# Block-sparse attention and SwiGLU feed-forward on one core: one fixed-order pipeline of key-tile steps in place of head-by-head attention

## The chip, the cores and the metric

The kernel runs on one core of one Trainium2 chip. The metric is the device time in microseconds (us) of one execution. TensorE is the matmul engine (PE in the profile, its weight loads PEld), VectorE is DVE, ScalarE is ACT, GpSimd is POOL. A "step" below is one key tile of 128 keys for one pair of heads and one half (384) of a batch's queries; there are 192 of them. A unit is the 24 steps of one such half batch; there are eight, and the feed-forward of a unit runs during the next one. A bank is a slice of PSUM, the memory that matmuls write to; each product below is written to one bank. A column tile is 32 or 64 of the array's 128 columns, used as a small array with weights of its own. A one-hot matmul has weights that are 1 in one column and 0 elsewhere, so that it sums its moving side into one chosen row. "Half rate" means matmuls at twice their later spacing.

In the feed-forward, gp and vp are the gate and the value product of one of 12 blocks f of d_ff; th is tanh of gp, u or uu is th and gp combined, hp is uu times vp, yp is the output projection and yo its copy. In the changed kernel o_ is the output product of a pair, zw the tile of sums, and norm_a to norm_d are the parts of the normalisation; FHL holds its factors.

## The reference

Attention with a block mask, then RMS norm and a SwiGLU feed-forward over the heads' joined output. Cut to what matters:

```python
B, H, S, D = 4, 8, 768, 64            # fp32 inputs; mask in 32x32 blocks
mask = |blk_i - blk_j| <= 1 | first/last block row or column | 3 sampled blocks per block row
attn = softmax(where(mask, q @ k.T / 8, -1e9));  x = (attn @ v) as [3072, 512]
xn  = x / sqrt(mean(x*x, -1) + 1e-6) * rms_g
out = (silu(xn @ w_gate) * (xn @ w_val)) @ w_out    # d_ff = 1536
```

## The kernel before

Per head, the scores come transposed (keys on partitions), the mask rides along as 24 more rows of K and Q, exp goes to SBUF, and the output product has the exp tile as weights and V with a column of ones as the moving side: 65 columns, of which the last is the softmax sum. The feed-forward (FFN) of batch b-1 is emitted between the heads of batch b. The framework's scheduler decides each engine's order.

```python
# pst (scores): 2 banks; pt: 2; po: 1; pff: gp, vp, yp one bank each
def attn_pair_load(b, hp):
    ...                                       # q, k: fp32 DMA in rows of 256 bytes, cast on VectorE
    for e, (raw_, bf) in enumerate(((qraw, qbf), (kraw, kbf))):
        ...
        for c in range(NC):
            nc.tensor.transpose(out=t_[:, c, :], in_=bf[:, c, :], identity=ident)
        nc.vector.tensor_copy(out=dst[0:D, sl0, :], in_=t_[0:D]...)       # both copies on VectorE
        nc.vector.tensor_copy(out=dst[0:D, sl1, :], in_=t_[64:128]...)

def attn_head(b, h, stage, e):
    for jt in range(NC):
        for ic in range(2):
            nc.tensor.matmul(out=stp, lhsT=KTf[0:64 + NB, sl, jt...], rhs=QTf[0:64 + NB, sl, ic...])
            nc.scalar.activation(out=ExpS[...], in_=stp, func=AF.Exp, scale=SCALE)   # 384 columns
    for it in range(NC):
        for jt in range(NC):
            nc.tensor.matmul(out=opsum[:, it, 0:65], lhsT=ExpS[... 128 wide], rhs=Vp[:, sl, jt, :], ...)
    ...                                       # 1/z, scaling, sums of squares on VectorE

def ffn_gateval(pool, g, f):                  # one gp bank, one vp bank during attention
    ...  # 4 matmuls to gp, 4 to vp
    nc.scalar.activation(out=th, in_=gp, func=AF.Tanh, scale=0.5)
    nc.vector.scalar_tensor_tensor(out=u, in0=th, scalar=1.0, in1=gp, op0=ALU.add, op1=ALU.mult)
    nc.vector.tensor_tensor(out=hp, in0=u, in1=vp, op=ALU.mult)
```

The softmax here doesn't subtract the row's maximum and nothing guards it: scores larger than these inputs give would overflow.

## Time and profile before

| | before |
|---|---|
| time, median | 436.8 us (436.0 to 437.4, 4 runs) |
| start, to the first score matmul | 54 us |
| batch 0, attention alone | 76 us |
| batches 1 to 3 with FFN | 253 us |
| last FFN, 768 tokens | 53 us |

The stretches view of the kernel before gives, for each stretch, its length, then busy time and instructions of each engine, the recorded TensorE clock, DMA share and GB/s. The clock reads 1.00 also where nothing was recorded, and the record of this trace begins only at 104.6 us, so the spacing of matmuls is the surer reading:

```profile
0.00:54.00 54.00, 5.74 (x42) 4.01 (x43) 14.69 (x43) 6.61 (x2) 6.17 (x19) 1.00 1.07 192
54.00:130.00 76.00, 64.52 (x481) 37.53 (x481) 36.60 (x156) 50.76 (x111) 0.00 (x0) 0.88 0.66 129
130.00:383.00 253.00, 241.25 (x2072) 141.88 (x2094) 168.12 (x574) 167.70 (x374) 0.00 (x0) 1.00 0.12 36
383.00:437.00 54.00, 48.72 (x267) 26.35 (x265) 27.03 (x49) 16.58 (x31) 0.00 (x0) 0.96 0.08 30
```

In the third stretch TensorE is busy 95% of the time: it is the bound there. In the first it does almost nothing. The last row ends 0.8 us after the span of 436.2 us. The timeline shows what the start waits for, and the DMA line of the page shows the small packets:

```profile
26.86 0.56 DVE L207 CAST qbf<-qraw 128x768 bf16<-128x768 f32 x1 [23.53 <-DMA qraw<-in_q_dram]
49.62 5.40 ACTq L127 DMA_DIRECT2D QTf<-Qmask  x6
54.31 0.80 PE L232 MATMUL stp<-QTf,KTf 88*128 88x384 bf16 x2 [3.37 <-DMA QTf<-Qmask]
...
DMA packets 82407, 30.80 MB, mean 71 GB/s; under 512 B 76452, under 2 KB 78276, under 8 KB 82372
```

The chain of waits (start, length, what) shows the same matmuls at two speeds, half rate during nearly all of batch 0 and full rate after it:

```profile
60.91 1.89 PE opsum L246 x31
70.88 0.64 PE stp L232 x2
...
140.44 1.08 PE opsum L246 x31
399.45 0.65 PE vp L157 x4
```

Two score matmuls of 384 columns take 0.64 us in batch 0; four value matmuls of 384 columns take 0.65 us later. The costliest groups of the page (busy us, mean ns of one, then idle time before and who ended it):

```profile
L238 ACT ACTIVATE ExpS<-stp 128x384 bf16<-128x384 f32 x384 | 171.1, 491 | 48.4 <-PE stp L232 33.8
L246 PE MATMUL opsum<-Vp,ExpS 128*128 128x65 bf16 x1152 | 76.8, 209 | 1.4 <-ACT ExpS L238 1.2
```

### The profile page before, as it was taken

The page shows a single profiled execution, that of the slowest core. Times are in us where ns is not written, and L with a number is a line of the kernel's source. Part 1 is how long each engine was busy: PE and PEld are TensorE (multiplying, and loading weights), DVE is VectorE, ACT ScalarE, POOL GpSimd, SP SyncE. Part 2 cuts the span into 40 slices and gives each one's busy share as a digit, 9 for nine tenths or more (in the row PEclk, how much of TensorE's full clock was granted, in tenths as well). Part 3 has the DMA queues.
Part 4 walks back from the last instruction along what each step waited for, and adds up shares of the span by engine and source line. Part 5 has one row for each costly group of instructions (what it writes and reads, how often), then busy time and mean ns, then how long its engine had stood idle before and what let it go on. Part 6 is the DMA issues. An engine that isn't in the chain of part 4 may idle for free.

```text
span 436.2 us, 7564 instructions
## 1 busy us (share of the span) xinstructions
PE 360.2 (83%) x2854; PEld 209.8 (48%) x2880; DVE 246.4 (56%) x821; ACT 241.7 (55%) x518; POOL 6.2 (1%) x19
## 2 busy tenths in 40 slices
PE   0002288898879999999999999989999999789996
PEld 0001134554555654655555555546555555345552
DVE  0016534363476862766887648578665566657380
ACT  0003266667676666676777476767773867333331
POOL 5000000000000000000000000000000000000000
PEclk9999999999659999999999999999999999989999
DMA  7999986557470202211310111010001000100101
GB/s 124 208 203 207 221 165 136 99 107 148 90 146 20 54 23 90 62 29 44 94 30 20 44 53 34 2 50 24 2 2 50 24 2 2 73 2 0 74 0 72
DMA packets 82407, 30.80 MB, mean 71 GB/s; under 512 B 76452, under 2 KB 78276, under 8 KB 82372
## 3 DMA queue, kind: packets, MB, share of 16 engines
q1 hardware_dynamic: 79332, 25.18, 26.1%
q0 software_dynamic: 2608, 4.72, 5.9%
q10 hardware_dynamic: 432, 0.44, 0.4%
q8 instruction: 22, 0.36, 0.4%
q14 instruction: 13, 0.11, 0.1%
HBM read 28.31 MB, written 6.29 MB: 79 GB/s over the span
## 4 chain that ended last, share of the span: by engine, by line
PE 71%; ACT 9%; SPq 8%; DVE 7%; DMA 3%; issue 2%; ACTq 0%; DVEq 0%
PE stp L232 17%; PE gp L151 14%; PE vp L157 13%; PE yp L175 13%; PE opsum L246 11%; ACT ExpS L238 7%; SPq L220 3%; SPq L202 3%; PE tqk L213 2%; PE to L280 2%; SPq L199 1%; DVE junk L259 1%; DMA vraw<-in_v_dram 1%; ACT yo L181 1%; DMA QTf<-Qmask 1%
## 5 line engine op out<-in xcount | busy, mean ns | idle before, releaser
L238 ACT ACTIVATE ExpS<-stp 128x384 bf16<-128x384 f32 x384 | 171.1, 491 | 48.4 <-PE stp L232 33.8
L232 PE MATMUL stp<-QTf,KTf 88*128 88x384 bf16 x384 | 126.5, 365 | 15.4 <-ACT ExpS L238 9.4
L165 DVE SCALAR_TENSOR_TENSOR u<-th,gp 128x384 bf16<-128x384 bf16 x96 | 53.0, 552 | 58.9 <-ACT th L163 56.5
L246 PE MATMUL opsum<-Vp,ExpS 128*128 128x65 bf16 x1152 | 76.8, 209 | 1.4 <-ACT ExpS L238 1.2
L246 PEld LDWEIGHTS <-ExpS 128*128 128x128 bf16 x1152 | 56.5, 107 | 44.3 <-issue 24.6
L163 ACT ACTIVATE th<-gp 128x384 bf16<-128x384 f32 x96 | 47.1, 490 | 54.2 <-PE gp L151 53.9
L175 PE MATMUL yp<-wo,hp 128*128 128x512 bf16 x262 | 65.6, 379 | 3.2 <-ACT yo L181 2.6
L169 DVE TENSOR_TENSOR hp<-u,vp 128x384 bf16<-128x384 bf16 x96 | 52.8, 551 | 19.3 <-PE vp L157 12.8
L232 PEld LDWEIGHTS <-KTf 88*128 88x128 bf16 x384 | 39.0, 107 | 30.5 <-issue 14.5
L151 PEld LDWEIGHTS <-wg 128*128 128x128 bf16 x384 | 35.8, 98 | 29.2 <-issue 7.9
L157 PEld LDWEIGHTS <-wv 128*128 128x128 bf16 x384 | 36.2, 98 | 25.2 <-issue 3.0
L213 PE MATMUL tqk<-ident,qbf 128*128 128x128 bf16 x96 | 13.0, 263 | 37.4 <-DVE qbf L207 37.3
L175 PEld LDWEIGHTS <-hp 128*128 128x128 bf16 x288 | 27.7, 97 | 32.2 <-issue 4.5
L181 ACT COPY yo<-yp 128x512 f32<-128x512 f32 x24 | 14.1, 586 | 42.7 <-PE yp L175 40.7
L259 DVE CUSTOM_DVE_ANT_0 junk<-stage,ssq 128x64 bf16<-128x64 bf16 x168 | 36.6, 277 | 0.3
L151 PE MATMUL gp<-xbr_152,wg 128*128 128x384 bf16 x96 | 31.6, 329 | 2.5 <-DVE u L165 1.7
L157 PE MATMUL vp<-xbr_152,wv 128*128 128x384 bf16 x96 | 31.6, 329 | 0.6 <-DVE hp L169 0.3
L151 PE MATMUL gp<-xbr_155,wg 128*128 128x384 bf16 x96 | 31.5, 329 | 0.1
L157 PE MATMUL vp<-xbr_153,wv 128*128 128x384 bf16 x96 | 31.6, 329 | 0.0
L151 PE MATMUL gp<-xbr_153,wg 128*128 128x384 bf16 x96 | 31.6, 329 | 0.0
L157 PE MATMUL vp<-xbr_154,wv 128*128 128x384 bf16 x96 | 31.4, 328 | 0.0
L157 PE MATMUL vp<-xbr_155,wv 128*128 128x384 bf16 x96 | 31.4, 328 | 0.0
(53 smaller groups left out, 235.0 us busy)
## 6 DMA issues: line engine op xcount, KB each, us to landing
qraw<-in_q_dram SPq DMA_DIRECT2D x32, 192.0 KB, 3.7
kraw<-in_k_dram SPq DMA_DIRECT2D x32, 192.0 KB, 4.0
vraw<-in_v_dram SPq DMA_DIRECT2D x32, 192.0 KB, 3.1
out_dram<-yo SPq DMA_DIRECT2D x24, 256.0 KB, 2.0
wg<-in_moe_w_gate_dram POOLq DMA_DIRECT2D x1, 1536.0 KB, 12.8
wv<-in_moe_w_val_dram POOLq DMA_DIRECT2D x1, 1536.0 KB, 18.8
wo<-in_moe_w_out_dram POOLq DMA_DIRECT2D x1, 1536.0 KB, 27.9
KTf<-Kind ACTq DMA_DIRECT2D x6, 36.0 KB
```

What stands on the lines that cost most here:

```text
L151: nc.tensor.matmul(out=gp, lhsT=wg[:, c, f * P:(f + 1) * P], rhs=xbr[c][:, g * TG:(g + 1) * TG], start=(c == 0), stop=(c == DM // P - 1),)
L157: nc.tensor.matmul(out=vp, lhsT=wv[:, c, f * P:(f + 1) * P], rhs=xbr[c][:, g * TG:(g + 1) * TG], start=(c == 0), stop=(c == DM // P - 1),)
L163: nc.scalar.activation(out=th, in_=gp, func=AF.Tanh, scale=0.5)
L165: nc.vector.scalar_tensor_tensor(out=u, in0=th, scalar=1.0, in1=gp, op0=ALU.add, op1=ALU.mult,)
L169: nc.vector.tensor_tensor(out=hp, in0=u, in1=vp, op=ALU.mult)
L175: nc.tensor.matmul(out=yp, lhsT=hprods[(g, f)][:, tt * P:(tt + 1) * P], rhs=wo[:, f, :], start=(f == 0), stop=(f == NF - 1),)
L181: nc.scalar.copy(out=yo, in_=yp)
L213: nc.tensor.transpose(out=t_[:, c, :], in_=bf[:, c, :], identity=ident)
L232: nc.tensor.matmul(out=stp, lhsT=KTf[0:64 + NB, sl, jt * P:(jt + 1) * P], rhs=QTf[0:64 + NB, sl, ic * 384:(ic + 1) * 384], start=True, sto ...
L238: nc.scalar.activation(out=ExpS[:, sle, jt * 2 + ic, :], in_=stp, func=AF.Exp, scale=SCALE,)
L246: nc.tensor.matmul(out=opsum[:, it, 0:65], lhsT=ExpS[:, sle, jt * 2 + it // 3, (it % 3) * P:(it % 3 + 1) * P], rhs=Vp[:, sl, jt, :], start ...
L259: nc.vector.tensor_tensor_reduce(out=junk, in0=stage[:, it, e, :], in1=stage[:, it, e, :], scale=1.0, scalar=(0.0 if h == 0 else ssq[:, b ...
```

## The change

The intent: load q, k, v in long rows and cast them in the DMA; run one exp over 768 columns (both heads of a pair) per step; make V the weights of the output product, so that 384 columns stream and the two heads of a pair fill two column halves of the array; take the softmax sums and the sums of squares by one-hot matmuls into 32-row column tiles; apply both normalisations in one multiply; put the FFN of the former 384 tokens between the steps, so that only 384 tokens are left at the end. A table of steps fixes the order on every engine. Core of the diff, cuts marked:

```diff
+    ctx.enter_context(tc.manual_schedule())            # every engine in emission order
+    ps_s = ...bufs=2   # two score buffers of two banks, lent to transposes and norms too
+    ps_a = ...bufs=1   # "zw" and "acc": sums; output product AND output projection
+    ps_f = ...bufs=1   # gp, vp
 ...
+    def load_w_chunk(i):                               # at steps 5, 9, 13, 17
+        for w, src, mul in ((wg, wgv, 1.0), (wv, wvv, 0.5)):
+            st = wst.tile([P, DM // P, FCH], FP32, name="wstage", tag="wstage")
 ...                                                    # chunk 0: a one-element memset of st on VectorE
+            nc.sync.dma_start(out=st, in_=src[:, :, f0:f0 + FCH])
+            for c in range(DM // P):
+                nc.vector.tensor_scalar(out=w[:, c, f0:f0 + FCH], in0=st[:, c, :],
+                    scalar1=gcol[:, c:c + 1], scalar2=mul, op0=ALU.mult, op1=ALU.mult)
 ...
+        t_ = ps_s.tile([P, 2, 1024], BF16, name="tqk", tag="s")
+        ...                                            # 24 transposes into two column tiles
+        nc.vector.tensor_copy(out=QTe[0:D, sl, :], in_=t_[0:D, 0, 0:S])
+        nc.scalar.copy(out=KTe[0:D, sl, :], in_=t_[0:D, 1, 0:S])
+        nc.vector.tensor_copy(out=QTo[D:P, sl, :], in_=t_[D:P, 0, 0:S])
+        nc.scalar.copy(out=KTo[D:P, sl, :], in_=t_[D:P, 1, 0:S])
 ...
+    def av(n): ...
+        for jt in range(NC):
+            for e in range(2):
+                nc.tensor.matmul(out=o_[64 * e:64 * e + 64, 0:TG],
+                    lhsT=vb[:, 2 * pr + e, jt * D:(jt + 1) * D], rhs=pt_[:, jt, e, :], ...)
+    def zsum(n): ...                                   # 12 matmuls, 4 column tiles
+                    nc.tensor.matmul(out=zwt[u][32 * c:32 * c + 32, :], lhsT=Ez[:, pr, :], ...)
 ...
+        if u == NU - 1:                                # last unit: gate and value in one tile
+            gv = ps_s.tile([P, 2, 512], FP32, name="gv", tag="s")
+            gp = gv[:, 0, 0:TG]
+        ...                                            # th, uu as before
+        vp = ps_f.tile([P, TG], FP32, name="vp", tag="vp") if gv is None else gv[:, 1, 0:TG]
 ...
+    LAG = 8
+        at(s1 + 1, av, n); at(s1 + 2, zsum, n); at(s1 + 4, wsum, n)
+            at(s1 + 4, norm_a, u); at(s1 + 5, norm_b, u); at(s1 + 6, norm_c, u)
+            at(s1 + 7, norm_d, u, 0); at(s1 + 7, norm_d, u, 1)
 ...
+            credit += RATE                             # FFN items spread over the steps by cost
```

## The prediction

> **What bounds the kernel now.** The stretches view cuts the 436.2 us span into four stages.
> (1) 0 to 54 us: TensorE does almost nothing (PE 8.5 of the first 58 us). The timeline shows why: the first qraw is cast at 26.9 us and the first score matmul starts at 54.3 us, behind loads in 256-byte rows (76,452 of 82,407 packets are under 512 B) and behind the mask rows, which go out by DMA at 49.6 us.
> (2) 54 to 130 us: attention of batch 0 alone. Matmuls run at half rate: two score matmuls in 0.64 us, 31 opsum matmuls in 1.89 us; later these cost 0.162 us each and 1.0 us.
> (3) 130 to 383 us: three batches of attention with FFN, about 84 us each, PE 96 to 98% busy.
> (4) 383 to 436 us: FFN of 768 tokens alone, dense (0.65 us per four 384-column matmuls, 0.216 us per yp matmul).
>
> **What the change does to TensorE work.** At the full rate, before needs FFN 187 us, scores 62, opsum 1152 x 0.032 = 37, transposes 16: about 302 us. After keeps the first two. Each AV matmul now streams 384 columns into 64 output rows (384 matmuls), the softmax sums are 384 one-hot matmuls of 32 rows, plus 32 square sums, more transposes (384 of half width) and normalisation matmuls. My estimate rests on column tiles running side by side; the Trainium skill, "TensorE: Matmul & The Clock Gate", Part 3, gives 2.38x for three column tiles; no run here shows it yet. Then AV is about 34 us, the sums 18 + 5, transposes 14, the rest 9: 329 us in all, 27 us MORE than before. Unpaired, it would be about 400 us.
>
> **What it removes.** The start: loads become 1,536-byte rows and the mask rows are copied on chip; I expect the first exp at 12 us instead of 55 (-42). Batch 0 alone: 32 steps, limited by ScalarE (one exp of 768 columns, about 0.75 us from 0.49 for 384 and 0.586 for 512 columns, plus KT and osb copies) and by VectorE, which scales weights in order behind 1.5 MB chunk loads: I expect about 47 us instead of 76 (-29). The tail is half as long: after the last score step, about 41 us including the rest of the former unit, the last norm chain and 23.4 us of FFN. ssq (junk 40 us, accumulator reads 15 us of DVE), the rstd multiply and Sqrt with its table loads (1.28 us each) go, but these were off the critical path in stage 3.
>
> **What it gives back.** In the mixed stage (160 steps) TensorE needs about 1.6 us per step, against the equivalent of 1.5 before. I add 0.25: drains when tile sizes change (skill, "TensorEngine Tiling (Array Packing)", Key Properties; not seen here), single gp and acc banks in a fixed order (gp, tanh 0.49, u 0.55 make a loop of some 2.2 us per f, wanted every 2.3), and score buffers lent to transposes and norms. 1.83 x 160 = 293 us.
>
> Sum: 12 + 47 + 293 + 41 = 393 us.
>
> **What would show it.** Timeline: first exp near 12 us; first tanh near 60; last exp near 350. AV pairs start within some ns of each other, 12 in about 1.1 us, 12 sum matmuls in about 0.6. ACT exp about 0.75 us x192. Stretches: PE over 90% busy from 70 to 350 us. Small packets nearly gone.
>
> **What would make it wrong.** Column tiles running one after another (+65 us: same or slower). Half rate lasting past step 32. VectorE blocked longer by weight chunks. Stalls in the mixed stage of 0.1 us per step are worth 16 us either way.
>
> Chances: faster 0.90, within 2% 0.06, slower 0.04. Eight in ten: 366 to 422 us.

## The result, and the profile after

The changed kernel is correct and slower: 488.95 us (487.49 to 490.25, 4 runs) against 436.78 us (436.01 to 437.44, 4 runs). The ratio is 1.12 (95% interval 1.117 to 1.123). Ratios here are the mean time of one kernel's fast runs over that of the other's of the same rounds, so they are not quite the ratios of the medians quoted.

The stretches of the changed kernel, cut where the first exp starts, where the first tanh (the first FFN work) starts and where the last exp ends:

```profile
0.00:16.50 16.50, 3.27 (x29) 1.76 (x30) 8.97 (x23) 2.87 (x3) 14.36 (x37) 1.00 0.72 95
16.50:82.90 66.40, 39.78 (x278) 16.23 (x277) 29.10 (x77) 33.36 (x45) 15.12 (x22) 0.77 0.65 149
82.90:425.90 343.00, 302.04 (x2211) 152.21 (x2209) 128.02 (x254) 203.91 (x316) 41.80 (x53) 0.98 0.17 32
425.90:488.00 62.10, 40.75 (x217) 19.54 (x215) 19.46 (x39) 11.24 (x23) 1.68 (x2) 0.97 0.07 26
```

Set against the sum in the prediction (12 + 47 + 293 + 41), every stage is longer: 16.5, 66.4, 343.0 and 61.8 us. The start did get much shorter, and small packets are nearly gone. In the mixed stage TensorE stands at 88% busy, and no engine is full. (The clock record begins at 27.2 us here and at 26.2 us in x_fence below, so the 1.00 of the first row says nothing.)

The arithmetic itself behaves as predicted. In the timeline (start, length, instruction), one pair's 12 output matmuls (o_, L262) start at 206.57 and the next matmul at 207.66, 1.09 us later; the 12 sum matmuls (zw, L280) take 0.60 us to the next start:

```profile
206.57 1.17 PE L262 MATMUL o__2023<-pt,vb 128*64 128x384 bf16 x12
207.66 0.82 PE L361 MATMUL gp<-xn,wg 128*128 128x384 bf16 x4
209.40 0.67 PE L280 MATMUL zw<-pt,Ez 128*32 128x384 bf16 x12
210.00 0.82 PE L361 MATMUL gp<-xn,wg 128*128 128x384 bf16 x4
...
DMA packets 22786, 24.02 MB, mean 49 GB/s; under 512 B 1764, under 2 KB 19684, under 8 KB 22756
```

One after another, 12 matmuls of 384 columns would take 12 x 0.1625 = 1.95 us. So the column tiles do run side by side.

What fills the rest of the time is waiting. The waits view (who for whom: total us, times, longest):

```profile
DVE uu L367 <- ACT th L365: 114.8, 96, 6.8
ACT KTe L231 <- DVE QTe L230: 36.2, 16, 11.6
PE gp L361 <- DVE uu L367: 18.9, 35, 2.0
PE gv L375 <- DVE uu L367: 14.0, 12, 1.2
PE s__421 L245 <- ACT KTo L233: 12.4, 1, 12.4
```

Here are three places in the timeline. First, batch 0. VectorE works in order; at 30.74 its one-element memset lets the next chunk's DMA go (issued at 30.83), and then it stands for 6.15 us until that chunk lands. The mask rows and the QTe copy, which the next scores need, sit behind it, and TensorE stands for 12.38 us:

```profile
30.74 0.06 DVE L210 MEMSET wstage<- 1x1 f32 x1
36.95 1.41 DVE L213 TENSOR_SCALAR wv<-wstage,gcol 128x384 bf16<-128x384 f32 x4 [6.15 <-DMA wstage<-in_moe_w_val_dram]
38.39 0.35 DVE L157 COPY KTe<-Kind 32x768 bf16<-32x768 bf16 x1
...
40.30 0.55 DVE L230 COPY QTe<-tqk 64x768 bf16<-64x768 bf16 x1
42.30 0.79 ACT L233 COPY KTo<-tqk 64x768 bf16<-64x768 bf16 x1 [0.63 <-DVE QTo L232]
43.15 0.48 PE L245 MATMUL s__421<-QTe,KTe 88*128 88x384 bf16 x1 [12.38 <-ACT KTo L233]
```

Second, the mixed stage. A pair's four copies run strictly one after another, hopping between two engines. ScalarE is in order too, so from 212.57 to 214.78 it serves only the two KT copies and the hops; a gate product that had started at 212.54 gets its tanh at 214.81, and the scores of 213.35 get their exp at 215.19:

```profile
211.99 0.55 DVE L230 COPY QTe<-tqk 64x768 bf16<-64x768 bf16 x1
212.57 0.79 ACT L231 COPY KTe<-tqk 64x768 bf16<-64x768 bf16 x1 [0.52 <-DVE QTe L230]
213.40 0.56 DVE L232 COPY QTo<-tqk 64x768 bf16<-64x768 bf16 x1 [0.86 <-ACT KTe L231]
213.99 0.79 ACT L233 COPY KTo<-tqk 64x768 bf16<-64x768 bf16 x1 [0.63 <-DVE QTo L232]
214.81 0.49 ACT L365 ACTIVATE th<-gp 128x384 bf16<-128x384 f32 x1
215.19 0.81 ACT L249 ACTIVATE pt<-s__2127 128x768 bf16<-128x768 f32 x1
```

Third, the tail. The value matmuls of the last unit wait for uu, though uu reads only the gate half of the tile and they write the other half. A block f of the FFN takes 2.63 us (447.74 to 450.37), where before took 1.3 us:

```profile
447.74 0.49 ACT L365 ACTIVATE th<-gv 128x384 bf16<-128x384 f32 x1 [2.14 <-PE gv L361]
448.26 0.56 DVE L367 SCALAR_TENSOR_TENSOR uu<-th,gv 128x384 bf16<-128x384 bf16 x1 [0.62 <-ACT th L365]
448.87 0.81 PE L375 MATMUL gv<-xn,wv 128*128 128x384 bf16 x4 [1.17 <-DVE uu L367]
449.52 0.81 PE L361 MATMUL gv<-xn,wg 128*128 128x384 bf16 x4
...
450.37 0.49 ACT L365 ACTIVATE th<-gv 128x384 bf16<-128x384 f32 x1 [2.14 <-PE gv L361]
```

### The profile page after: what moved, and what is told of

It is laid out like the page before. It is cut to its first block, busy times and chain, and to the rows that moved or that the text cites. A ratio compares the mean times of both kernels' runs of the same rounds, so it can differ in the third digit from the quotient of the medians.

```text
span 487.7 us, 6743 instructions
## 1 busy us (share of the span) xinstructions
PE 385.8 (79%) x2730; PEld 189.7 (39%) x2730; DVE 185.6 (38%) x392; ACT 251.4 (52%) x385; POOL 73.0 (15%) x112
## 4 chain that ended last, share of the span: by engine, by line
PE 57%; DVE 15%; ACT 15%; issue 5%; DMA 4%; POOL 2%; POOLq 0%; ACTq 0%; DVEq 0%
PE gp L361 11%; PE yp L389 11%; PE vp L375 7%; DVE uu L367 5%; ACT th L365 5%; PE zw L280 4%; ACT pt L249 3%; ACT KTe L231 3%; DMA wstage<-in_moe_w_val_dram 3%; PE tqk L227 2%; PE gv L375 2%; ACT KTo L233 2%; DVE QTo L232 2%; DVE QTe L230 2%; PE gv L361 2%
## 5 line engine op out<-in xcount | busy, mean ns | idle before, releaser
L367 DVE SCALAR_TENSOR_TENSOR uu<-th,gp 128x384 bf16<-128x384 bf16 x84 | 46.5, 554 | 104.0 <-ACT th L365 104.0
L361 PE MATMUL gp<-xn,wg 128*128 128x384 bf16 x336 | 70.0, 331 | 18.9 <-DVE uu L367 18.9
L375 PE MATMUL vp<-xn,wv 128*128 128x384 bf16 x336 | 69.9, 331 | 1.3 <-DVE hp L378 1.3
L378 DVE TENSOR_TENSOR hp<-uu,vp 128x384 bf16<-128x384 bf16 x84 | 46.6, 554 | 25.5 <-PE vp L375 19.0
L375 PEld LDWEIGHTS <-wv 128*128 128x128 bf16 x384 | 35.6, 98 | 46.9 <-issue 26.5
L245 PEld LDWEIGHTS <-KTo 128*128 128x128 bf16 x192 | 19.4, 101 | 42.8 <-issue 30.8
L231 ACT COPY KTe<-tqk 64x768 bf16<-64x768 bf16 x16 | 12.7, 792 | 36.2 <-DVE QTe L230 36.2
L245 PEld LDWEIGHTS <-KTe 88*128 88x128 bf16 x192 | 19.6, 102 | 26.3 <-issue 10.3
L262 PEld LDWEIGHTS <-vb 128*64 128x64 bf16 x384 | 21.0, 117 | 21.4 <-issue 13.7
L280 PE MATMUL zw<-pt,Ez 128*32 128x384 bf16 x384 | 22.2, 338 | 0.0
L345 DVE TENSOR_TENSOR xn<-osb,fb 128x768 bf16<-128x768 f32 x16 | 14.8, 952 | 16.7 <-PE fb L342 16.6
```

The lines of the kernel that those rows point to most:

```text
L231: nc.scalar.copy(out=KTe[0:D, sl, :], in_=t_[0:D, 1, 0:S])
L245: nc.tensor.matmul(out=s_[:, e, 0:TG], lhsT=KT[0:K, sl, jt * P:(jt + 1) * P], rhs=QT[0:K, sl, ic * TG:(ic + 1) * TG], start=True, stop=True)
L262: nc.tensor.matmul(out=o_[64 * e:64 * e + 64, 0:TG], lhsT=vb[:, 2 * pr + e, jt * D:(jt + 1) * D], rhs=pt_[:, jt, e, :], start=(jt == 0), s ...
L280: nc.tensor.matmul(out=zwt[u][32 * c:32 * c + 32, :], lhsT=Ez[:, pr, :], rhs=pt_[:, 2 * j2 + par, e, :], start=(pr == 0 and j2 == 0), stop ...
L361: nc.tensor.matmul(out=gp, lhsT=wg[:, c, f * P:(f + 1) * P], rhs=xns[u][:, c, :], start=(c == 0), stop=(c == NP - 1))
L367: nc.vector.scalar_tensor_tensor(out=uu, in0=th, scalar=1.0, in1=gp, op0=ALU.add, op1=ALU.mult)
```

## The experiments

Unless it says otherwise, each is one edit to the changed kernel ("after"). All used 3 rounds beside the kernel before on the same chip, and all results are correct except one that is wrong. The stages are read from each trace: first exp; from there to the first tanh; from there to the end of the last exp (mixed); the tail. The last column but one is the trace's span in us; the ratio is to the kernel before, as in the result. A gain in us given below is the difference of two such ratios times 436.7 us, which takes out the small differences between chips. Gains of 3 us are near what these runs can tell: in e4_spread and e10_gpcopy, whose edits act from step 32 on, the exp of step 21 already comes 2.6 and 2.5 us earlier than in the changed kernel.

In e5_norm and the x_ runs the FFN starts two steps later, so some 3 us that the other rows count as mixed stand in their second stage. From the exp of step 32 to the last one, which is the same cut for all, it is 343.8 us in the changed kernel, 324.5 in e5_norm, 324.2 in e9_copies, 308.7 in x_manual, 300.9 in x_hybrid and 301.1 in x_fence.

| kernel | first exp | to first tanh | mixed | tail | span | ratio |
|---|---|---|---|---|---|---|
| predicted | 12 | 47 | 293 | 41 | 393 | |
| after | 16.5 | 66.4 | 343.0 | 61.8 | 487.7 | 1.120 |
| e1_tail | 16.5 | 66.4 | 342.7 | 49.9 | 475.5 | 1.093 |
| e2_auto | 34.6 | 54.8 | 307.4 | 45.2 | 442.0 | 1.017 |
| e3_weights | 16.5 | 50.0 | 345.5 | 61.7 | 473.7 | 1.088 |
| e4_spread | 16.5 | 63.3 | 332.8 | 70.2 | 482.8 | 1.112 |
| e5_norm | 16.5 | 64.6 | 320.5 | 58.7 | 460.3 | 1.061 |
| e7_sums | 16.5 | 62.5 | 333.3 | 61.4 | 473.7 | 1.097 |
| e8_auto_w | 23.7 | 54.4 | 307.4 | 43.5 | 429.0 | 0.987 |
| e9_copies | 15.8 | 64.0 | 323.6 | 60.0 | 463.4 | 1.070 |
| e10_gpcopy | 16.5 | 64.0 | 348.4 | 58.1 | 487.0 | 1.121 |
| e11_all_act | 14.9 | 59.0 | 345.8 | 60.1 | 479.8 | 1.108 |
| e12_warm | 16.5 | 61.8 | 343.5 | 60.1 | 481.9 | 1.113 |
| x_manual | 15.8 | 44.4 | 304.5 | 46.9 | 411.6 | 0.948 |
| x_hybrid | 15.8 | 56.7 | 296.5 | 42.6 | 411.6 | 0.945 |
| x_manual10 | 15.8 | 46.1 | 321.4 | 55.1 | 438.4 | 1.008 |
| x_fence | 15.8 | 44.6 | 297.1 | 42.5 | 400.0 | 0.922 |

### e1_tail: the last unit's value product in its own tile

```diff
-        vp = ps_f.tile([P, TG], FP32, name="vp", tag="vp") if gv is None else gv[:, 1, 0:TG]
+        vp = ps_f.tile([P, TG], FP32, name="vp", tag="vp")
```

> One edit to the changed kernel: in the last unit the value product goes to a bank and tile of its own instead of the second half of the gate's tile. Theory (false wait): after the last score step each of the 12 feed-forward columns takes 2.63 us because the value matmuls wait for VectorE's uu, which reads only the gate half; with its own tile a column takes about 1.35 us, so about -15 us (489 to about 474 us), and the wait of the value matmuls for uu goes. Rival (the tail is slow because one f's chain of tanh, uu, hp is 2.6 us long whatever the tile): no change.

Measured: 477.2 us, 12 us less, all of it in the tail. The wait for uu is gone. In its timeline the blocks alternate between 1.46 us (449.86 to 451.31) and 1.83 us (451.31 to 453.14), 1.64 on the mean in place of 2.63; in every second one the value product waits for hp, which frees the single vp bank. That is why 12 came and not 15:

```profile
449.86 0.81 PE L375 MATMUL vp<-xn,wv 128*128 128x384 bf16 x4 [0.37 <-DVE hp L378]
450.50 0.81 PE L361 MATMUL gv<-xn,wg 128*128 128x384 bf16 x4
451.31 0.81 PE L375 MATMUL vp<-xn,wv 128*128 128x384 bf16 x4
```

So the wait was a false one: two halves of one tile, in two banks, were ordered as if they overlapped.

### e2_auto: the fixed order given up

```diff
-    ctx.enter_context(tc.manual_schedule())
+    pass
```

> One edit to the changed kernel: the fixed order is given up, the framework's own scheduler orders each engine as it did in the kernel before; same instructions. Theory (the stalls come from the fixed order running into single-buffered PSUM banks, 81 us of TensorE waiting in the mixed stage against 38 before): 25 to 60 us faster than the changed kernel, 430 to 465 us. Rival (the new arithmetic itself, more TensorE work and more tile-mode switches, costs the time): within 2% of the changed kernel, 489 us.

Measured: 444.3 us, 45 us less, as the theory said. By stage: the mixed stage is 36 us shorter, the tail 17 and the second stage 12, while the first exp comes 18 us later, because the scheduler fetches weights first. The same arithmetic in another order costs within 2% of the kernel before. This rules out that the new arithmetic is what cost 52 us; it doesn't say yet which part of the order did.

### e3_weights: weights cast by DMA and scaled late

```diff
-            st = wst.tile([P, DM // P, FCH], FP32, name="wstage", tag="wstage")
...          # the memset of chunk 0 goes too
-            nc.sync.dma_start(out=st, in_=src[:, :, f0:f0 + FCH])
+            nc.gpsimd.dma_start(out=w[:, :, f0:f0 + FCH], in_=src[:, :, f0:f0 + FCH])
...          # the scaling, in place, moves to scale_w_chunk
-        at(5 + 4 * i, load_w_chunk, i)
+        at(5, load_w_chunk, i)
+        at(26 + 2 * i, scale_w_chunk, i)
```

> One edit to the changed kernel: the gate and value weights are cast by DMA straight into their final tiles and issued at step 5, and VectorE scales them in place at steps 26 to 32 instead of waiting for staged chunks at steps 5 to 17. Theory (VectorE, in order, sits behind weight chunks, so QT and mask copies of the next pair come late and the score matmuls stand 22 us): the first tanh moves from 83 us to about 60 us and the time falls by about 20 us to 468 us. Rival (batch 0 is paced by half-rate TensorE and by score buffers lent to transposes): the first tanh stays after 75 us and the time falls by less than 8 us.

Measured: 475.3 us, 14 us less. The first tanh comes at 66.5 us instead of 82.9, and the other stages don't move by more than 3 us. The theory holds at three quarters of its size: 16 us of the second stage were VectorE held by weights, waiting for chunks and scaling them, in front of what the scores needed. By the starts of the exps, 10.3 of the 16 us come at step 10 and 5.1 at step 16, next to TensorE's stands of 12.4 and 7.2 us in the changed kernel.

### e4_spread: output projection between the next unit's gate and value products

```diff
+            if f % 2 == 1 and ys:
+                items.append(ys.pop(0))          # a half y tile of unit u-1
...  # and an open y tile is finished first when an output product comes
```

A first form without the last line deadlocked when it was built (the output product waits for the shared bank, whose y tile ends later in the same order).

> One edit to the changed kernel: the six output-projection halves of a unit are put between the gate and value products of the next unit, one after every second f, so a new gate product comes every 2 steps instead of every 1.33. Theory (the one gp bank, whose loop of matmul, tanh behind an exp, and uu is 2.2 to 2.6 us): TensorE's waits for uu in the mixed stage fall from 25 us to under 8 us and the time by 12 to 20 us, to about 472 us. Rival (those waits only stand in front of ScalarE's queue, which is the true limit): the waits move to exp or tanh and the time stays within 1%.

Measured: 485.6 us, 3.5 us less. The mixed stage is 10.2 us shorter and the tail 8.4 us longer: the edit puts a unit's output projection off to the next unit, so 24 more gate and value matmuls and at least 14 more of yp lie after the last exp, about 7 us of TensorE work that was moved and not saved. I worked out TensorE's waits in the mixed stage from the trace (start-to-start time above the full-rate spacing, put to the semaphore that came last): those of the gate product for uu fell from 25 to about 13 us, but those of the output product for yo, at the shared "acc" bank, rose from 2.5 to 11 us. The theory that the gp bank is the limit was half wrong: the wait moved on.

### e5_norm: the normalisation one step later

```diff
-    LAG = 8
+    LAG = 10
-            at(s1 + 6, norm_c, u);  at(s1 + 7, norm_d, u, 0);  at(s1 + 7, norm_d, u, 1)
+            at(s1 + 7, norm_c, u);  at(s1 + 8, norm_d, u, 0);  at(s1 + 9, norm_d, u, 1)
```

> One edit to the changed kernel: the second part of the normalisation (norm_c) comes one step later, its broadcast halves one and two steps later, and the feed-forward of the unit starts two steps later. Theory (TensorE, in order, stands in front of norm_c for the eight small VectorE steps and a 0.87 us power on GpSimd, some 8 us in the mixed stage, plus 5 us at the broadcasts, and a stand of that length is followed by half-rate windows of 3.4 us): the waits for FHL fall from 10 us to under 5 us, and the time by 5 to 13 us. Rival (the chain is longer than one more step, or half rate has another cause): less than 3 us.

Measured: 462.1 us, 26 us less, twice what was expected. The wait that was named did go: TensorE's stands in front of norm_c, in the changed kernel and then here (who for whom: total us, times, longest):

```profile
PE ft L328 <- DVE FHL_192 L321: 6.7, 4, 2.5
PE ft L328 <- DVE FHL_193 L321: 4.0, 3, 1.5
PE ft L328 <- DVE FHL L321: 2.6, 2, 1.7
```

To see where the time went, I took the starts of the 192 exps in both traces and summed, over the mixed stage, how much shorter each of the 24 steps of a unit became. At steps 6 to 9 of a unit, where the norm sits, 9.9 us were gained (5.5 and 15.6 at steps 6 and 7, 11.2 given back at 8 and 9); the other 9.4 us of that sum lie at other steps, as gains and losses that mostly cancel. The edit moves the whole FFN two steps against transposes and output products, so it changes more than the norm. The norm's own steps hold 10 us; why the new meeting of FFN and attention is better by as much again stays open. Part of both is half rate: up to the last exp the record has 6.8 us of it after the first tanh, the changed kernel 17.1, and at some 1.4 us for a window of 3.4 us (see e12_warm) that is an estimate of 4 us.

### e7_sums: a third of the sum matmuls (wrong result)

```diff
-        for j2 in range(NC // 2):
+        for j2 in range(1):
```

> Wrong result on purpose: only 4 of the 12 one-hot sum matmuls of each pair are issued. Theory (the new arithmetic is cheap because four column tiles run side by side; the time goes in waits): 256 fewer matmuls save 32 x 0.33 us = 11 us at most, and less where other waits take the place: 4 to 11 us. Rival (the sums and the mode switches around them cost what was lost): over 25 us.

Measured: 478.2 us, 10 us less (relative error 0.03, as intended: the softmax sums are incomplete). That is the array time of the 256 matmuls and no more. The rival falls as to the sums: they are not where the time went. The switches between tile sizes stay in this run, since four of the twelve matmuls of each pair still run; that these don't make the loss either is shown by e2_auto and x_fence, which keep all of them.

### e8_auto_w: e1, e2 and e3 together

> Three edits to the changed kernel together: the order left to the scheduler, the weights cast by DMA and scaled late, the value product of the last unit in its own bank. Theory (the causes add up: order 45 us of which the scheduler lost 18 us again at the start by fetching weights first, weights 14 us, tail already cured by the order): first exp near 17 us instead of 34.6 us, and the time 412 to 428 us, faster than the kernel before (437 us). Rival (the scheduler's late start overlapped with work that has to be done anyway): 435 to 445 us.

Measured: 430.6 us, 1.3% below the kernel before, just outside both ranges. The first exp came at 23.7 us, not at 17, and the first tanh at 78.1 against 66.5 in e3_weights: the scheduler still mixes later work into the start. The mixed stage is as in e2_auto.

### e9_copies: the KT copies on VectorE

```diff
-        nc.scalar.copy(out=KTe[0:D, sl, :], in_=t_[0:D, 1, 0:S])
+        nc.vector.tensor_copy(out=KTe[0:D, sl, :], in_=t_[0:D, 1, 0:S])     # KTo likewise
```

> One edit to the changed kernel: the two KT copies of a pair go to VectorE like the QT copies, so that the four copies out of the lent score buffer no longer hop between two engines and ScalarE loses 25 us of copies. Theory (the four copies run one after another, 3.5 us per pair with the hops, and keep one of two score buffers from the scores; 2.4 us on one engine): 4 to 12 us faster. Rival (the lent buffer is hidden behind feed-forward work in the mixed stage and only the weights stall stage 2): within 3 us.

Measured: 465.7 us, 22 us less, twice what was expected. The same comparison of exps by step is plain here. This is my own sum, in us gained over the mixed stage, by the step's place in a unit of 24 steps; transposes stand at places 3, 9, 15 and 21:

```
step of the unit:   3     9     15    21    | all 20 others
gained:            4.3   5.6   5.0   4.3    | 0.4
```

The gain stands where a pair is transposed (12 pairs in the mixed stage), but the 0.4 hides gains and losses that cancel. At the step after, 3.0 us are given back at place 22 and 2.1 at place 10, so that 13.7 us, 1.1 us a pair, stay with the transposes. Of the other 5.9 us most lie at places 5, 6, 11 and 17, and the changed kernel's record has half-rate windows at 5, 6, 7, 11 and 16, where this run's has one in all, at place 7 (see e12_warm). TensorE's own waits for KTo were only 2.3 us in the mixed stage; the rest had been charged to others, uu, hp and exp among them, which would follow if ScalarE was held and tanh and exp came late. The four copies now follow each other on VectorE, and ScalarE goes on with exps, at 213.03 and 215.70:

```profile
213.82 0.55 DVE L230 COPY QTe<-tqk 64x768 bf16<-64x768 bf16 x1 [2.90 <-PE tqk L227]
214.30 0.54 DVE L231 COPY KTe<-tqk 64x768 bf16<-64x768 bf16 x1
214.85 0.56 DVE L232 COPY QTo<-tqk 64x768 bf16<-64x768 bf16 x1
215.33 0.55 DVE L233 COPY KTo<-tqk 64x768 bf16<-64x768 bf16 x1
```

### e10_gpcopy: gp copied out by VectorE at once

```diff
+        gs = ffw.tile([P, TG], BF16, name="gs", tag="gs")
+        nc.vector.tensor_copy(out=gs, in_=gp)
-        nc.scalar.activation(out=th, in_=gp, func=AF.Tanh, scale=0.5)       # uu likewise
+        nc.scalar.activation(out=th, in_=gs, func=AF.Tanh, scale=0.5)
```

> One edit to the changed kernel: VectorE first copies gp to SBUF as bf16, and tanh and uu read the copy, so the one gp bank is free 0.65 us after its last matmul instead of after tanh and uu; 96 more VectorE copies of about 0.55 us. Theory (TensorE waits for the gp bank because tanh stands behind an exp in ScalarE's queue): its waits for uu at the gate product, 25 us in the mixed stage, fall under 5 us and the time by 12 to 25 us. Rival (as the spread run hinted, taking one bank wait away only brings the next one, or more VectorE work delays hp): less than 6 us.

Measured: 489.5 us, no change; the mixed stage is 5 us longer. The gate product's waits at its bank did fall, from 25 to 5 us, but the value product's waits for hp rose from 2 to some 27 us. The gp theory falls: the bank was only where a chain that is too late shows up. Freeing the first of two banks of the chain moves the wait to the second, and the chain got longer by a copy.

### e11_all_act: all four copies on ScalarE

```diff
-        nc.vector.tensor_copy(out=QTe[0:D, sl, :], in_=t_[0:D, 0, 0:S])
+        nc.scalar.copy(out=QTe[0:D, sl, :], in_=t_[0:D, 0, 0:S])            # QTo likewise
```

> The mirror of the copies run: all four copies of a pair on ScalarE, so ScalarE has about 25 us MORE copies than in the changed kernel but they no longer hop between engines. Theory (what cost 22 us was ScalarE standing in order between the hops, 46 us of waits of KTe and KTo for VectorE, with the next exp and tanh behind it): faster than the changed kernel by 5 to 18 us in spite of the load. Rival (ScalarE's load of copies is what cost): slower than the changed kernel by 5 us or more.

Measured: 482.5 us, 5.5 us less (some 3 us either way by the two intervals), at the low end of the theory's range. By stage, the first exp comes 1.6 us earlier and the second stage is 7.4 us shorter; the mixed stage got 2.8 us longer. So hops by themselves don't decide the mixed stage. What the two copy runs have in common is the time for which ScalarE can serve neither exp nor tanh: 2.2 us per pair in the changed kernel (212.57 to 214.78), 3.0 us here (from the first copy to the end of the last), none in e9_copies. That fits both, but so does the theory of e9_copies: the lent score buffer is held, from a pair's first transpose to its last copy, for 3.70 us in the changed kernel, 3.89 here and 2.97 in e9_copies. The runs don't separate the two.

### e12_warm: six useless matmuls in front of norm_c

```diff
+        for _ in range(6):
+            nc.tensor.matmul(out=ft, lhsT=ident, rhs=Wm, start=True, stop=True)
```

> One edit to the changed kernel: six matmuls of no use (0.97 us) are put in front of norm_c's matmuls, in the time in which TensorE stands waiting for FHL; their result is overwritten. The chain is as long as before. Theory (a part of the norm run's 25 us was the half rate that followed a stand of over 1.2 us, some 17 us of half-rate windows in the mixed stage, worth 8 us): fewer windows, 2 to 8 us faster. Rival (the windows have another cause, or the six matmuls only add work): 0 to 6 us slower.

Measured: 484.4 us, 3 us less, inside the expected range, but barely clear of the noise and not for the expected reason. The gain lies before the first tanh (61.8 against 66.4 us), and 2.8 us of it are there at step 21, before the first of the new matmuls at step 30. The mixed stage is the same within 0.5 us, and half-rate windows after the first tanh went only from 20.5 to 17.1 us: they moved and did not go. So the run doesn't test what it was made for, but it shows what a window costs. The changed kernel's at 180.8 and 235.4 us are missing, and the steps that they lie in are 1.6 and 1.3 us shorter; two others came, at 241.5 and 255.2 us, and cost 1.4 and 1.3 us. And in units 4 to 7 (counted from 0) the step at place 7 takes 4.90 us, but 6.19 in the one for which a window is recorded: unit 4 in the changed kernel, unit 5 in e9_copies. Five windows in the changed kernel's mixed stage are then worth some 7 us, an estimate.

### x_manual: e1, e3, e5 and e9 together, still in fixed order

> Four edits together, still in fixed order: value product of the last unit in its own bank (12 us alone), weights late (14), norm one step later (25), all four copies on VectorE (22). If the causes add up: 489 - 73 = 416 us. If they partly cured the same waits and half-rate windows, as I think since the last two cured far more than the waits they name: 420 to 435 us. If over 440 us, the single gains were the same gain seen four times.

Measured: 413.8 us, ratio 0.948: 75 us below the changed kernel, 5% below the kernel before. The single gains (12 + 14 + 26 + 22 = 74 us) add up fully, so no two of these edits cured the same wait to a size that shows, and my doubt about overlap was wrong. Among the hundred longest lines of its waits view none is of a KTe or KTo copy waiting for another engine, and no half-rate window is recorded between the first tanh and the last 0.4 us.

### x_hybrid: x_manual's edits, fixed order up to step 32 only

```diff
-    ctx.enter_context(tc.manual_schedule())
+    first_part = ExitStack(); first_part.enter_context(tc.manual_schedule())
+        if step == 32:
+            first_part.close()
```

> The same four edits, with the fixed order only up to step 32 and the scheduler's order after it. Theory (the fixed order is good at the start, where the scheduler lost 7 to 18 us, and bad in the mixed stage, where it loses 25 to 35 us): first tanh before 68 us, mixed stage about 305 us, end at 405 to 420 us, faster than the kernel before by 4% or more. Rival (the mixed stage of the fixed order was slow from the four causes alone, so nothing is left for the scheduler): equal to the four edits in fixed order within 1%.

Measured: 413.4 us, equal to x_manual as the rival said, but not for the rival's reason; of the theory the end came true, and the first tanh before 68 us did not (72.5). The mixed stage is 8 us shorter and the tail 4; the first tanh comes 12 us later, since the scheduler put later work into the start.

### x_manual10: x_manual and the gp copy of e10

> The four edits in fixed order plus the copy of gp. Theory: the gp bank is the largest wait left, so 10 to 20 us below the four edits alone, 400 to 420 us. Rival (VectorE, now with KT copies and gp copies, becomes the limit): no gain, and hp shows up as the wait of TensorE.

Measured: 440.2 us, 26 us worse than x_manual. The rival holds: in the mixed stage the value product's waits for hp are about 29 us, against 3 us in x_manual.

### x_fence: x_hybrid with a fence at step 32

```diff
+            tc.no_sync_barrier()                 # nothing is ordered across step 32
```

> The four edits, fixed order up to step 32, scheduler's order after it, and a fence at step 32 so that the scheduler can't mix later work into the start (in the run without the fence the first tanh came at 72.5 us instead of 60.2, and the mixed stage took 296.5 us instead of 304.5). Theory: first tanh near 61 us, mixed stage 295 to 300 us, end at 400 to 407 us. Rival (the early work that the scheduler mixed in has to be done anyway, so the mixed stage gets longer by as much): 410 to 415 us.

Measured: 401.5 us (401.3 to 401.8), ratio 0.922 (0.919 to 0.926), correct: 7.8% faster than the kernel before and the best of all. The theory holds at each stage. Its stretches, cut in the same way:

```profile
0.00:15.80 15.80, 3.31 (x29) 1.76 (x30) 9.14 (x23) 1.31 (x2) 13.71 (x34) 1.00 0.69 91
15.80:60.40 44.60, 37.29 (x291) 16.14 (x290) 28.06 (x83) 29.77 (x41) 22.05 (x32) 0.92 1.08 162
60.40:357.50 297.10, 295.61 (x2195) 147.31 (x2194) 138.89 (x278) 182.77 (x289) 41.90 (x52) 1.00 0.18 36
357.50:400.00 42.50, 38.11 (x219) 19.54 (x219) 19.86 (x40) 11.23 (x22) 1.67 (x2) 0.98 0.10 38
```

TensorE is busy for 295.61 of 297.10 us in the mixed stage, where the changed kernel had 302.04 of 343.00.

## Why the prediction was wrong

**Right: what bounds the kernel before, the packets, the column tiles, TensorE's need.** The trace shows 1.09 us for 12 output matmuls and 0.60 us for 12 sum matmuls ("about 1.1" and "about 0.6"). The Trainium skill, "TensorE: Matmul & The Clock Gate", Part 3, on which this rested, gives 2.38x for three column tiles; four here ran 12 matmuls in 0.60 us instead of 1.95 us, about 3.2x, switches of tile size included. The need of about 1.6 us per step was right too: counting the full-rate spacing of each recorded matmul, with the 1.09 and 0.60 us of the groups, gives about 264 us for the 160 steps, 1.65 us each. And e7_sums shows that the sums cost what was priced.

**Wrong: "I add 0.25" per step for the mixed stage.** The mixed stage took 343.0 us, not 293, so the allowance should have been about 0.5 us per step. This is the largest failed term, 50 of 95 us: the allowance for waits was half of what they took, while TensorE's own need was right. The prediction named the suspects in one line ("single gp and acc banks in a fixed order ..., score buffers lent to transposes and norms") and then gave them a flat sum. It looked at TensorE's banks and followed no queue through. The hopping copies of a pair cost 13.7 us at their steps (e9_copies, 19.4 us of the mixed stage in all); whether they do so by holding ScalarE for 2.2 us, with the next exp and tanh behind, or by holding the lent score buffer is not separated. norm_c stands in TensorE's queue one step too early (e5_norm: 19.3 us from step 32 on, of which 10 at the norm's own steps). Half-rate windows, which the prediction listed as a danger, are some 7 us by estimate, in part inside these two gains. At the same cut, from step 32 on, x_manual takes 35 us less than the changed kernel in fixed order, and x_fence, which also leaves the order after step 32 to the scheduler, 43 us less. Its mixed stage of 297 us (301 from step 32) shows that the predicted 293 was nearly right for a kernel without these waits.

**Wrong: "about 47 us" for batch 0.** It took 66.4 us. The prediction knew that VectorE "scales weights in order behind 1.5 MB chunk loads" and listed "VectorE blocked longer by weight chunks" among the things that would make it wrong; the term was mis-sized by 19 us. e3_weights gives 16 of them back, and x_manual, with the copies moved as well, takes 44.4 us.

**Wrong: "about 41 us" for the tail.** It took 61.8 us. The last unit's FFN stood in the sum at its dense time, 23.4 us (its banks looked doubled; the prediction doesn't say so). The false wait between two halves of one tile made each of 12 blocks 2.63 us long; e1_tail gives 12 us of it back and x_fence 19.

**Wrong by little: the first exp**, 16.5 us instead of 12. The chain before it holds the mask rows, six VectorE copies from 10.85 to 13.1 us, and then the four hopping copies, to 15.9 us.

Sum of the misses: 4.5 + 19.4 + 50.0 + 20.8 = 94.7 us, which is 487.7 - 393. Every term came out longer than it was put, and together they outweigh the expected gain of 44 us.

**What stays open:** half of what e5_norm gained in the mixed stage (9 of 19 us in the comparison by step, perhaps some of it half rate), and whether the copies cost through ScalarE or through the lent score buffer. e10_gpcopy, x_manual10 and e4_spread show that those waits can't be read as the cost of the bank where they appear.

## What to carry to other kernels

When an order is fixed by hand, an in-order queue that stands for one late thing delays everything behind it, and the loss shows up as waits elsewhere: before accepting a flat allowance, follow each engine's queue through one period and ask what sits in front of its next critical instruction. Keep data waits (weights still on their way) and short copies out of the queues that feed the bottleneck, and give two products that are used at different times two tiles. A cheap comparison is the start times of the same repeated instruction in two traces, step by step: it shows where a gain lies, where the waits view only shows where it was charged. It also shows a gain at steps that the edit can't have touched, and such a gain is not the edit's.

## What the Trainium skill lacked or had wrong

- "TensorEngine Tiling (Array Packing)", Key Properties, says that changing the tiling mode drains TensorE, without a cost. In this trace a switch goes with about 0.1 us each way: from the second score matmul (206.31) to the first output matmul (206.57) 0.26 us instead of 0.16, and 1.09 us for 12 output matmuls whose array time is 12 x 0.1625 / 2 = 0.98 us. That the drain is what takes it is not shown.
- "TensorE: Matmul & The Clock Gate", Part 1, ties the fall to half rate, in its table of states, to an idle window of about 3.4 us; its paragraph on short idles between groups of matmuls gives them no length. In the changed kernel the record shows half-rate windows of 3.4 us (at 126.1, 180.8, 235.4, 351.4 and 365.1 us) after single stands of only 0.8 to 2.0 us in otherwise busy stretches (for instance 1.73 us before norm_c at 180.96).
- The same part says that a busy window of about 3.4 us releases full rate, but not how unbroken it has to be. In the kernel before, TensorE was busy 43.9 of 50.6 us from 54 to 104.6 us, for at most 4.7 us without a break of 0.1 us or more, and stayed at half spacing all the while (0.64 us for two 384-column matmuls). The clock record begins only at 104.6 us. The page does warn that these records can be unreliable; the spacing of matmuls is the safer reading.
- No page says that a wait may be put between two halves of one PSUM tile in two banks though the data don't overlap; here it cost 12 us (e1_tail).
